# Sinkhorn attention with a leaky FFN: 96 short products ahead of q, fewer gap products, loads in halves, and a new order

## The chip, the cores and the metric

The kernel runs on one core of one Trainium2 chip. The metric is the device time in microseconds, as the median of several executions; less is better. The engines are PE (TensorE), ACT (ScalarE), DVE (VectorE), POOL (GpSimd) and SP (SyncE), and they run side by side. PE issues a weight load and a product for each matmul, and POOL and SP also issue the DMAs.

## The reference

Four batches of eight heads, 768 positions and 64 features go through an attention in which each block of 96 queries looks at one block of keys that has been mixed from all eight blocks by a normalised 8 x 8 matrix P. The result, 3072 tokens of 512 features, goes through a two-layer network with a leaky activation.

```python
P = sort_net                                   # (4, 8, 8, 8)
for _ in range(5):
    P = P - max(P, -1); P = exp(P)
    P = P / (sum(P, -1) + 1e-9)
    P = P / (sum(P, -2) + 1e-9)
k_sorted = einsum('bhij,bhjcd->bhicd', P, k_blocks)   # the same for v
scores = (q_block @ k_sorted_block.T) / sqrt(64)
attn = softmax(scores)
x = (attn @ v_sorted_block) -> (3072, 512)
h = x @ w_in                                   # 512 x 2048
g = max(h, 0) + alpha * min(h, 0)
out = g @ w_out                                # 2048 x 512
```

## The kernel before

**The work.** The 32 pairs of batch and block are called groups g (eight groups to a batch). For batch 0, q and k are turned by small PE products of 64 columns (pairs, L541; k is mixed with P in the same product through the matrix BDK), v is first copied into a padded layout (conv_v, L571, copies at L375) and then mixed (prep_v, L582), all in units that are copied out of PSUM by ACT or DVE. The matrix BDK comes from the sinkhorn steps on DVE and ACT (L490 to L505) and from spread (L514 to L527). A group of attention is: first scores (L617), row maxima on DVE (L623), for batch 0 second scores with the maxima subtracted (L638, L629), exponentials on ACT (L650, or L661 for batch 0), outputs (L672), division on DVE (L679, L682), and a transpose into xT (L697 on PE for batch 0, a DMA else). Then ffn1 (L719) multiplies xT with one of 16 tiles of w_in, ACT and DVE apply the activation (L729, L732), and ffn2 (L758) multiplies with w_out, 128 tokens at a time, in four parts; the result is copied to outstg (L375) and written out. The FFN works on chunks of two, two and then four groups.

**Loads.** They are DMAs that POOL issues, all in one queue: q, k and v of batch 0 (load_q L400, load_kv L422), w_in in four pieces of 128 rows (L793), w_out in two (L798), then what later batches need. A load converts f32 to bf16.

**The order.** Every step is put into a graph with an estimated duration, a priority and what it depends on. A list scheduler with a model of the engines then fixes the order of every engine; each engine runs its list strictly in that order. ORDER is a table with two characters for each step that shift its priority; it was found by a search.

**Gap products.** After the scheduling, `fill` walks through PE's list. Where the model sees PE idle ahead of a step, it puts products of the identity with itself there, whose results nobody reads (warm, L877). It does so in three stretches, up to the first ffn2. One such product has 256 bf16 columns and counts as 108 ns:

```python
n = int((op.start - begin) * 0.9 / unit)
if op.start <= hi and n > 0:
    x = _Op("pe", lambda e, n=n, bank=bank: make(e, n, bank), n * unit, ...)
```

The lines are those of the profile.

Of the kernel before, what the change touches and what calls it, by code (L numbers as in the profile page):

```python
# [7 lines left out]
AP = bass.AP  # L8
# [19 lines left out]
TILE_NS = 95  # L28
ORDER = (
    "W0W0W0W0W0W0W0W05GW0l3T78PEQ1K9l7Y65EIEs4XMvOvAlRW0mdJRwEqG4iGXTQOfufwMuee8gGT6cGbXokEJe4B90JCveHZicAA9jUQB1DzPFF4GGKaHc"  # L30
    "8aPHCA4nBAfy6_mlSHVedcjZcmmXi2fOu5noSXO0p4bQmukgg7JLd5XNb4k5NyqRpxOAKOZpWHdU9UOeaEbWQSrkh3-4smk4t4aqO11GW0bWNrrYNUK2Em3W"
    "2-AR7c4nBTOyEx6nE6VTT3j4j_VCppjHttlwZvlfv-kVjdpxgA_GempJzTIedlrBmB-4g0hyzlNlESMRb36rHveUTSSo_DJxhukpJSN1RQJPWXRw7D7NPepN"
    "QEhEy-6LVV39A485D4GZRj9GDA3061FN4n5GEbTSGINERVBKI9Ft7O2iRp59KrE4gJRCMWDaCESFPvKjTt9wZzLl482x11A0Da1F1NId1X4T6Q7b0m4DTr4g"
    "2i1g1eN0OeCWfkODTu5Z2C0m0m6NCN0m1r457q5cGFMvcfHJHoL_KsLa8wGqPdSBZuA_CCAIwDZHjf0mwrsWdxmhmkNeWavmxaDELyOyrUFK2lDPdQ78mbQb"
    "WuvsGKVUU6Nd-XkcdKgTYGtvjwNTp9zqg3yppVD9CnuRzjsWmqpjTvylWL2-w_ClQ0iJecrHjXVv8R9HiPVlTeWB4Z99MmHqDAu5513h5ekV4Diu363k6kJQ"
    "rZSUN2nBcMssxIy6a_v8XLqyqGhIPfj7OGV3XGhW1oogFOaIDH8o0mJVtiJxKqAp3N9JMY1sY_hrX9C4EHFH3BArWvqF3M98H4D89jGTHhINHEF_Dvf5SDFn"
    "rSSkUD3rACBFS1XdtyJ92D319yKv4PAqLpgfOu6E8oeoybjzDa7169FkRzft5Y9UOJ8hlIVreecmrQgn4HDsI9SaI0izJ56w3uW6DR1Y38MbAM8XKaJ44L7J"
    "Y7UVjbB3LoG8H5N8YZXrYHTnSaxmiheb5aGQDOQI6GXS95ZXBsJ4BFPAMBe_BAMxEPVlG9jCHM3_WfNkBp3V9WPO8baR9yGwzkzueeMe38MCadIUXl5Qcs7J"
    "DOBlN-Gn7gL14HDlT8Ez3fEPB18w9wQiIkJEFpFADrC1lvWrTZj8KzFRNf7ddav8_GsjmEakOMoYtjyUg1YMl4yry1S6stxphKsUfUqV78aYBOmolzOHlkw8"
    "Mb-biXpg895_a5RvUqk2L45-Fec_n9HPKxZCPjvWRO58F9668Ye5JUSEM26xOC3-J2JGYaSvWWfhbbQNr-sKcSPWnA_Gds_G_GiK_GpwF_ghbQPUoTSS_Gsc"  # L40
    "q4S7WnvGsUdDhK21AG4z4mGeJr9EDSIrI5RwjLKpaXL9VY3F1K1N49molEoJm119U7Amo1DbO2KKl_AYYJgfRnnEgdcwOKVxqGCPkOtLkUvryOdGph_Gj8oL"
    "udQtU3umL1WoqYTwDytNbVnVG4npnGydlwoTRPqoK25XDXGB-5rkQrL8nGpEfObklbqMUYRdMj1FMPw9SxSjdQjos7XA9WToxOntFhJ_baHhgAoXeE5R1CAq"
    "oFABUOeBHKpvWeLBcpEZ_GtJLTpVTtWIrhaEgUPZEaBFS82PEPHUFfgPdYab_4awxrhWcBexo9zxvQnrpoZYPPBx9GjLv8WhywsJ-lhx-q-t-e-ByhSbt5gx"
    "q4PEDZFbnI4QFE4k3BLt6gEHcrF6ZL1Mfhc1vgZZMQcqYuBOYI_G_GTzQOEg9EIBNH5XA7MNAH2Q9ELq1J1v553_429_7N3F0m1g6g2JUvpMJxdjNGBQSSS1"
    "H_8zbrJn1xGE3wC06DBVBG96C85Q991aHaExFVOv6pA0Cu4v7N6E6J8DAO8d96IRWcDNJ5ZF3QMTfEWUGJYABk9ZE6t9HmMG_GSVw6gnroXjyAeUdRuvVyy_"
    "YvtFRRysp0bzdEjry3ylvWu6cbpWohxbOirASrmYtQEWQAmUyk7-9_qA6aAYAxQnDBSEn8w9V1vVKHbZkJwWjzK7yrToFljrlArn3TFsgw5LBKXJlvd2nqMQ"
    "Oc6xyqlhhuQ2LQ0m303l-muwxUYcej_Gzw-nur_G_C-lq9ellKA9x8y5pUP1NYsOmosT-KqwnXejbfwxxDiNq6UfNwuZVmx7d4BBi6qqQ-BHzD-E-Cy7xRox"
    "rAtnbRIPl2WJONciriI2IXCIyydAq1pzpjhfvfeetzdHgVdvipuskrXTkovejtqSuhn7p8ybyvx-wrvprDrrwiwxxJx_z7v9vyzWoXuBxFq9qFzEy1xuyLtZ"
    "vM"
# [20 lines left out]
class _Op:  # L70
    __slots__ = ("eng", "fn", "dur", "prio", "deps", "dma", "idx", "pos", "inc", "start", "end",
                 "users", "left", "ready", "turn", "engs", "tiles")

    def __init__(self, eng, fn, dur, prio, dma, idx):
        self.eng, self.fn, self.dur, self.prio, self.dma, self.idx = eng, fn, dur, prio, dma, idx
        self.deps = set()
        self.turn = set()
        self.users = []
        self.inc = None
        self.engs = eng  # L80
        self.tiles = (0, 0)


class _Graph:
# [7 lines left out]
    def add(self, eng, fn, dur, r=(), w=(), prio=0.0, dma=None, tiles=(0, 0)):  # L92
        op = _Op(eng, fn, dur, prio, dma, len(self.ops))
        op.tiles = tiles
# [19 lines left out]
    def span(self, op, e, at, loads):  # L114

        if op.dma is None:
            d = op.dur[e] if isinstance(op.dur, dict) else op.dur
            if e == "pe":
                if op.tiles[0] and not loads[2]:
                    d += TILE_NS  # L120
                loads[2] = op.tiles[1]
            return at + d, at + d
# [22 lines left out]
    def schedule(self):  # L145
# [17 lines left out]
        loads = [0.0, 0.0, 0]  # L163
# [39 lines left out]
    def fill(self, make, unit, spans):  # L203

        out, last = [], 0.0
        for op in self.order["pe"]:
            for lo, hi, deps, bank in spans:
                begin = max([last, lo] + [self.ops[d].end + 300 for d in deps])
                n = int((op.start - begin) * 0.9 / unit)
                if op.start <= hi and n > 0:  # L210
                    x = _Op("pe", lambda e, n=n, bank=bank: make(e, n, bank), n * unit, 0.0, None, len(self.ops))
                    x.start, x.end = begin, begin + n * unit
                    x.deps.update(deps)
                    self.ops.append(x)
                    out.append(x)
# [77 lines left out]
def bass_sinkhorn_attn__then__act_prelu_kernel(  # L293
# [94 lines left out]
    d_k = [dma_sem("k%d" % n) for n in range(7)]  # L388
    d_v = [dma_sem("v%d" % n) for n in range(7)]
# [29 lines left out]
    def load_kv(t, src, name, sem, g, b, prio):  # L419
        n = 4 if b == 3 else 1  # L420
        for x in range(n):
# [3 lines left out]
                load_us / n, r=paced(g, x) * (b == 3), w=[(name, b % 2), (name, b % 2, x)] if x == 0 else [(name, b % 2, x)],  # L425
                prio=prio, dma=(sem[b + x], 700 * (b == 3 and name == "KS")))
# [7 lines left out]
    def consts():  # L434
# [25 lines left out]
        for n in range(NE):  # L460
# [13 lines left out]
              r=["identf"], w=["selk"], prio=-66)  # L474
# [33 lines left out]
    def spread(bs, prio):  # L508
# [7 lines left out]
        G.add(PE, f, 100 * n, r=["Pb", "selk"] + [("xT", 1)] * (bs[0] > 0), w=PSP, prio=prio)  # L516
# [30 lines left out]
    def prep_q(u, prio, bank):  # L547
        t, off, row, keys = bank
        G.add(PE, pairs(QS[0], 0, u, identb, 0, 128, bank), 372, r=[("QS", 0), "identb"], w=keys, prio=prio, tiles=(1, 1))
# [4 lines left out]
    def prep_k(b, u, prio, bank=BANK_P):  # L554
        n = b % 2
        t, off, row, keys = bank
        G.add(PE, pairs(KS[n], n, u, BDK, b * 128, 512, bank), 372, r=[("KS", n)] + [("KS", n, x) for x in range(4)] + [("BDK", b)], w=keys,
              prio=prio, tiles=(1, 1))
# [9 lines left out]
    def conv_v(b, u, prio):  # L568
# [3 lines left out]
              r=[("VST", b % 2)] + [("VST", b % 2, x) for x in range(4)], w=[("VD", u)], prio=prio)  # L572

    def prep_v(b, u, prio, bank=BANK_P):
# [11 lines left out]
        G.add(PE, f, 374, r=[("VD", u), "VD0", ("BDK", b)], w=keys, prio=prio, tiles=(1, 1))  # L586
# [9 lines left out]
    def attention(g, prio):  # L596
# [14 lines left out]
        def s1(e):  # L611
            inst = None
            for h4 in range(4):
# [7 lines left out]
              w=banks_s, prio=ps_, tiles=(1, 1))  # L621
# [36 lines left out]
        else:  # L658
            G.add(PE, s2, 626, r=kt_keys + qt_keys + [("nm", m), "identb"],
                  w=banks_s, prio=ps_, tiles=(1, 0))  # L660
# [15 lines left out]
        op = G.add(PE, o, t_pe(*[(65, 65)] * 8), r=vs_keys + ([("ET", me), ("ETtail", me)] if far else [("Es0", m), ("Etail", m)]), w=banks_o, prio=prio)  # L676
# [24 lines left out]
        G.add(PE, tr, t_pe(*[(96, 128)] * 4), r=[("xq", me), "identb"], w=banks_o[:1], prio=prio)  # L701
# [7 lines left out]
    def ffn1(ga, gb, ft, prio):  # L709
# [6 lines left out]
        def f(e):  # L716
            inst = None
            for kt in range(KT_TILES):
# [5 lines left out]
        op = G.add(PE, f, t_pe(*[(n, 128)] * 4), r=[("xT", g % 16) for g in range(ga, gb)] + [("w_in", kt) for kt in range(KT_TILES)],  # L724
              w=keys, prio=prio)
# [15 lines left out]
    def ffn2(t, prios):  # L741
# [11 lines left out]
        for x, (bank, key) in enumerate(banks):  # L753
            for part in range(4):
                def f(e, part=part, bank=bank, x=x):
                    inst = None
                    for ft in range(4 * part, 4 * part + 4):
# [7 lines left out]
                           + [("w_out", part // 2)], w=key, prio=prios[part] + x)  # L765
# [26 lines left out]
    for kt in range(KT_TILES):  # L792
        G.add(POOL, lambda e, kt=kt: e.dma_start(  # L793
            AP(w_in_bf, kt * DFF, [[KT_TILES * DFF, 128], [1, DFF]]),
            AP(moe_w_in.tensor, kt * 128 * DFF, [[DFF, 128], [1, DFF]])),
# [126 lines left out]
```

## Time and profile before

| | |
|---|---|
| median of 3 executions | 249.22 us (248.56 to 250.04) |
| the profiled execution | 250.91 us, of which the span from first to last instruction is 249.2 us |
| PE busy | 233.1 us, 94% of the span, 2711 products |
| PE weight loads | 140.1 us, 56% |
| DVE busy | 168.3 us, 68% |
| ACT busy | 155.2 us, 62% |
| POOL busy | 48.9 us, 20% |
| mean granted clock of TensorE | 0.993 |
| DMA | 29.81 MB, mean 120 GB/s |
| L877 (gap products) on psYP | 85 products, 14.1 us busy |
| chain that ended last | PE 85%, DVE 6%, DMA 3%, issue 3%, ACT 2% |

Times in the profile count from the first instruction. A busy PE need not be PE at its peak, since products overlap and their ends are modelled. The clock row shows the share of the full clock that TensorE was granted. An idle time that the profile puts down to "issue" is one in which the engine waited for nothing that the profile shows. The durations of a row are means of one execution.

### The profile page before, as it was taken

Reading aid. Unit: us, or ns where it says so; the run is one execution under the profiler, and the core shown is the slowest. Engines: PE = TensorE matmul, PEld = TensorE weight load, DVE = VectorE, ACT = ScalarE, POOL = GpSimd, SP = SyncE. Lnnn points to the kernel's source line nnn. Section 1 sums busy time; section 2 is a strip of 40 time slices with the busy share of each in tenths; the row PEclk is TensorE's granted clock in tenths of the full one; section 3 lists DMA queues with packets and bytes.
Section 4 is the critical chain, followed back from the end, with each engine's and each line's share of the span. In section 5 each row is a group of like instructions: output and inputs, shape, how many; then the busy total and the mean of one; then the engine's idle time right before and its main releaser. Section 6 shows DMA issues by size and latency. Waiting matters only on the chain.

```text
span 249.2 us, 6548 instructions
## 1 busy us (share of the span) xinstructions
PE 233.1 (94%) x2711; PEld 140.1 (56%) x2742; DVE 168.3 (68%) x340; ACT 155.2 (62%) x422; POOL 48.9 (20%) x70
## 2 busy tenths in 40 slices
PE   4989798989899998999999999999999999999995
PEld 3767486667655555555555555554555555555544
DVE  5777566488877887765778687654866775655520
ACT  4447355588887886746677766557676476455511
POOL 8992000064751104960000000000000000000000
PEclk9999889999999999999999999999999999999999
DMA  5999999999699899994375443213443353002103
GB/s 102 206 214 208 175 211 170 211 206 171 63 123 178 153 147 176 159 168 73 88 123 115 112 92 89 59 35 93 105 105 85 62 141 92 16 0 87 43 10 117
DMA packets 66318, 29.81 MB, mean 120 GB/s; under 512 B 58592, under 2 KB 61936, under 8 KB 66288
## 3 DMA queue, kind: packets, MB, share of 16 engines
q0 software_dynamic: 23632, 13.63, 41.8%
q1 hardware_dynamic: 42656, 15.76, 32.2%
q8 instruction: 21, 0.34, 0.6%
q14 instruction: 9, 0.07, 0.1%
HBM read 27.28 MB, written 6.29 MB: 135 GB/s over the span
## 4 chain that ended last, share of the span: by engine, by line
PE 85%; DVE 6%; DMA 3%; issue 3%; ACT 2%; POOL 0%
PE psH L719 31%; PE psYP L758 28%; PE psYP L877 4%; PE psS L758 3%; PE psO L672 3%; PE psYP L582 3%; PE psS L617 3%; PE psYP L541 2%; DMA ET<-Esb 2%; DVE hT L732 2%; PE psS L629 1%; ACT t L729 1%; PE psS L638 1%; DVE VS L375 1%; PE psO L582 1%
## 5 line engine op out<-in xcount | busy, mean ns | idle before, releaser
L732 DVE SCALAR_TENSOR_TENSOR hT<-t,omaT,psH 128x384 bf16<-128x384 f32 (+1 forms) x139 | 77.7, 571 | 39.9 <-ACT t L729 38.4
L719 PE MATMUL psH<-xT,w_in_bf 128*128 128x384 bf16 (+1 forms) x556 | 98.6, 313 | 0.2 <-DVE hT L732 0.2
L729 ACT ACTIVATE t<-psH 128x384 f32<-128x384 f32 (+1 forms) x139 | 62.6, 463 | 45.4 <-PE psH L719 43.5
L758 PE MATMUL psYP<-w_out_bf,hT 128*128 128x512 bf16 x306 | 78.2, 379 | 3.6 <-DVE hT L732 1.2
L719 PEld LDWEIGHTS psH<-xT,w_in_bf 128*128 128x128 bf16 x556 | 50.3, 98 | 32.9 <-DVE hT L732 3.6
L650 ACT ACTIVATE Esb<-psS,nf 96x96 bf16<-96x96 f32 x192 | 46.1, 343 | 5.0 <-DVE nf L623 5.0
L758 PEld LDWEIGHTS psYP<-w_out_bf,hT 128*128 128x128 bf16 x336 | 30.4, 98 | 30.1 <-DVE hT L732 1.1
L623 DVE TENSOR_REDUCE nf<-psS 96x8 f32<-96x768 f32 x24 | 22.8, 949 | 5.5 <-PE psS L617 5.4
L375 POOL COPY VD<-VST 128x384 bf16<-128x384 bf16 x15 | 14.5, 966 | 39.0 <-DMA VST<-in_v_dram 32.7
L682 DVE TENSOR_TENSOR xq<-psO,rec 96x512 bf16<-96x512 f32 x31 | 21.3, 686 | 0.9
L404 POOL DMA_DIRECT2D QN<-in_q_dram x24 | 19.8, 850 | 0.9 <-DMA xT<-xq 0.5
L877 PE MATMUL psYP<-identb 128*128 128x256 bf16 x85 | 14.1, 319 | 3.4 <-ACT identb L375 3.4
L375 ACT ACTIVATE outstg<-psYP 128x512 f32<-128x512 f32 x14 | 8.4, 597 | 7.4 <-PE psYP L758 7.4
L375 ACT ACTIVATE VS<-psYP 112x512 bf16<-112x512 f32 x14 | 9.6, 684 | 5.1 <-PE psYP L582 5.1
L582 PEld LDWEIGHTS psYP<-BDK,VD 128*64 128x64 bf16 x416 | 8.6, 111 | 6.9 <-issue 2.7
L617 PE MATMUL psS<-KT,QTz 64*128 64x96 bf16 x248 | 10.8, 205 | 1.7 <-issue 1.7
L877 PEld LDWEIGHTS psYP<-identb 128*128 128x128 bf16 x85 | 9.0, 112 | 5.7 <-ACT identb L375 3.4
L582 PE MATMUL psYP<-BDK,VD 128*64 128x64 bf16 x416 | 11.5, 198 | 0.7 <-DVE VS L375 0.7
L679 DVE RECIPROCAL rec<-psO 96x8 f32<-96x8 f32 x31 | 6.2, 199 | 7.6 <-PE psO L672 7.2
L672 PEld LDWEIGHTS psO<-VS,ET 112*128 112x128 bf16 x192 | 8.6, 98 | 4.3 <-DMA ET<-Esb 0.8
L672 PE MATMUL psO<-VS,ET 112*128 112x65 bf16 x192 | 9.9, 194 | 0.9 <-DMA ET<-Esb 0.6
L617 PEld LDWEIGHTS psS<-KT,QTz 64*128 64x128 bf16 x248 | 6.2, 94 | 6.4 <-ACT t L729 3.1
(117 smaller groups left out, 179.2 us busy)
## 6 DMA issues: line engine op xcount, KB each, us to landing
out_dram<-outstg SPq DMA_DIRECT2D x23, 256.0 KB, 2.2
KS<-in_k_dram POOLq DMA_DIRECT2D x3, 768.0 KB, 33.4
VST<-in_v_dram POOLq DMA_DIRECT2D x3, 768.0 KB, 32.5
QN<-in_q_dram POOLq DMA_DIRECT2D x24, 96.0 KB, 5.5
w_in_bf<-in_moe_w_in_dram POOLq DMA_DIRECT2D x4, 512.0 KB, 17.6
w_out_bf<-in_moe_w_out_dram POOLq DMA_DIRECT2D x2, 1024.0 KB, 28.5
QS<-in_q_dram POOLq DMA_DIRECT2D x1, 768.0 KB, 7.1
VST<-in_v_dram POOLq DMA_DIRECT2D x4, 192.0 KB, 4.5
```

The costliest lines, as they stand in the source:

```text
L375: return e.activation(o, i, ACTF.Copy) if e is nc.scalar else e.tensor_copy(o, i)
L582: inst = e.matmul(AP(t, th * 64 * row + off + dd * 64, [[row, 64], [1, 64]]), AP(VD, (8 * u + dd) * 64, [[4096, 128], [1, 64]]), AP(BDK, b ...
L617: inst = e.matmul(o, AP(QTz[n], hp * 64 * QP + h4 * 768 + i * 96, [[QP, 64], [1, 128]]), AP(KT[n], hp * 64 * ld + (h4 * 8 + i) * bk, [[ld, ...
L623: G.add(DVE, lambda e: e.tensor_reduce(AP(nx, 0, [[8, 96], [4, 2], [1, 4]]), AP(psX, 0, [[1024, 96], [512, 2], [96, 4], [1, 96]]), AxisLis ...
L650: inst = e.activation(AP(Esb[me], p * 128, [[1024, 96], [64, 2], [1, 48]]), AP(psX, (p // 4) * 512 + (p % 4) * 96, [[1024, 96], [48, 2], [ ...
L672: inst = e.matmul(AP(psZ, hp * 512 + h4 * 68, [[1024, 128], [1, 65]]), AP(ET[me] if far else Es0[m], pos(h4, hp) * 96, [[800, nk], [1, 128]]),
L682: G.add(DVE, lambda e: e.tensor_tensor(out=AP(xq[me], 0, [[512, 96], [256, 2], [64, 4], [1, 64]]), in0=AP(psZ, 0, [[1024, 96], [512, 2], [ ...
L719: inst = e.matmul(AP(pt, poff, [[1024, 128], [1, n]]), AP(w_in_bf, kt * DFF + ft * 128, [[KT_TILES * DFF, 128], [1, 128]]), AP(xT, kt * XR ...
L729: G.add(ACT, lambda e: e.activation(AP(t1[tb], 0, [[384, 128], [1, n]]), AP(pt, poff, [[1024, 128], [1, n]]), ACTF.Relu, scale=-1.0), t_ac ...
L732: G.add(DVE, lambda e: e.scalar_tensor_tensor(out=AP(hT, ft * RING + tok % RING, [[FT_TILES * RING, 128], [1, n]]), in0=AP(t1[tb], 0, [[38 ...
L758: inst = e.matmul(AP(bank[0], bank[1], [[1024, 128], [1, n]]), AP(hT, ft * RING + tok % RING, [[FT_TILES * RING, 128], [1, 128]]), AP(w_ou ...
L877: inst = e.matmul(AP(t, off, [[row, 128], [1, 256]]), identb[:, :], AP(identb, 0, [[128, 128], [0, 2], [1, 128]]))
```

## The change

- **96 short products.** PE's list now begins with 96 products of a 32-column piece of the identity with 16 columns, as soon as the identity is there. The plan counts 2.7 us for them.
- **Gap products.** A gap product now has 512 columns. After 9 us of the plan, a gap takes first as many f32 products as fit (865 ns each), then bf16 ones (216 ns each); before 9 us only bf16 ones, at 480 ns each.
- **Loads.** load_kv loads batch 0 in two column halves, and since K and V share it, V as well as K. A unit of prep_k of batch 0 depends on its own half only; conv_v depends on all pieces. w_in is loaded in eight pieces, four row blocks by two column halves, and an ffn1 tile depends on its own column half.
- **The model.** Each PE step tells how many products it has (mms). The scheduler counts two instructions for each, and lets a step that passes a border of 256 instructions wait until 5500 ns (2500 ns after 36 us of the plan) after the border before.
- **The order.** ORDER is new throughout, and the copy into selk has another priority.

```diff
+FETCH = 256
+FETCH_NS = 5500
+FETCH0 = (205, 6100.0, 449)
 ORDER = (
...
@@ span
                 loads[2] = op.tiles[1]
+                loads[3] += 2 * op.mms
+                if loads[3] > loads[5]:
+                    loads[5] += FETCH
+                    late = loads[4] + (FETCH_NS if at < 36000 else 2500) - at
+                    if late > 0:
+                        d += late
+                    loads[4] = at + (late if late > 0 else 0)
             return at + d, at + d
...
-        loads = [0.0, 0.0, 0]
+        loads = [0.0, 0.0, 0, *FETCH0]
@@ fill
-        out, last = [], 0.0
+        out, last = [head], 0.0
+        head.idx = len(self.ops)
+        self.ops.append(head)
...
-                n = int((op.start - begin) * 0.9 / unit)
-                if op.start <= hi and n > 0:
-                    x = _Op("pe", lambda e, n=n, bank=bank: make(e, n, bank), n * unit, 0.0, None, len(self.ops))
-                    x.start, x.end = begin, begin + n * unit
+                left = (op.start - begin) * 0.9
+                n = 0 if begin < 9000 else max(int(left / 865), 0)
+                m = max(int((left - n * 865) / (480 if begin < 9000 else 216)), 0)
+                if op.start <= hi and n + m > 0:
+                    x = _Op("pe", lambda e, n=n, m=m, bank=bank: make(e, n, m, bank), 0, 0.0, None, len(self.ops))
+                    x.start, x.end = begin, begin + n * 865 + m * 216
@@ load_kv
-        n = 4 if b == 3 else 1
+        n = (2, 1, 1, 4)[b]
...
-                prio=prio, dma=(sem[b + x], 700 * (b == 3 and name == "KS")))
+                prio=prio + x / 100, dma=(sem[b + x + (b > 0)], 700 * (b == 3 and name == "KS")))
@@ prep_k
-        G.add(PE, pairs(KS[n], n, u, BDK, b * 128, 512, bank), 372, r=[("KS", n)] + [("KS", n, x) for x in range(4)] + [("BDK", b)], w=keys,
-              prio=prio, tiles=(1, 1))
+        G.add(PE, pairs(KS[n], n, u, BDK, b * 128, 512, bank), 372, r=[("KS", n, x) for x in ((u // 3,) if b == 0 else range(4))] + [("BDK", b)], w=keys,
+              prio=prio, tiles=(1, 1), mms=16)
@@ ffn1
-        op = G.add(PE, f, t_pe(*[(n, 128)] * 4), r=[("xT", g % 16) for g in range(ga, gb)] + [("w_in", kt) for kt in range(KT_TILES)],
-              w=keys, prio=prio)
+        op = G.add(PE, f, t_pe(*[(n, 128)] * 4), r=[("xT", g % 16) for g in range(ga, gb)] + [("w_in", kt, ft // 8) for kt in range(KT_TILES)],
+              w=keys, prio=prio, mms=4)
@@ main
-    for kt in range(KT_TILES):
-        G.add(POOL, lambda e, kt=kt: e.dma_start(
-            AP(w_in_bf, kt * DFF, [[KT_TILES * DFF, 128], [1, DFF]]),
-            AP(moe_w_in.tensor, kt * 128 * DFF, [[DFF, 128], [1, DFF]])),
-            2750, w=[("w_in", kt)], prio=-40 + kt, dma=(dma_sem("wi%d" % kt), 0))
+    for x in range(2):
+        for kt in range(KT_TILES):
+            G.add(POOL, lambda e, kt=kt, x=x: e.dma_start(
+                AP(w_in_bf, kt * DFF + x * 1024, [[KT_TILES * DFF, 128], [1, 1024]]),
+                AP(moe_w_in.tensor, kt * 128 * DFF + x * 1024, [[DFF, 128], [1, 1024]])),
+                1375, w=[("w_in", kt, x)], prio=-40 + 4 * x + kt, dma=(dma_sem("wi%d%d" % (kt, x)), 0))
...
+    def warm(e, n, m, bank):
         t, off, row, keys = bank
         inst = None
+        for x in range(n + m):
+            ident = identf if x < n else identb
+            inst = e.matmul(AP(t, off, [[row, 128], [1, 512]]), ident[:, :], AP(ident, 0, [[128, 128], [0, 4], [1, 128]]))
         return inst
+
+    def short(e):
+        inst = None
+        for _ in range(96):
+            inst = e.matmul(AP(psYP, 0, [[1024, 32], [1, 16]]), identb[:, :32], identb[:, :16])
+        return inst
+    head = _Op("pe", short, 0, 0.0, None, 0)
+    head.deps.add(ident_op)
+    head.start = G.ops[ident_op].end + 50
+    head.end = head.start + 2700
```

## The prediction

> **What bounds the kernel now.** I read the page first: PE is busy 94% of the span, and its rows for the slices from 100 us on are nines. By stretches of time PE is busy 138.46 of 140 us between 100 and 240, and 28.45 of 30 between 70 and 100. What can be won lies in the first 70 us, so I read the timeline of PE and the chain of waits there.
>
> ```profile
> PEclk9999889999999999999999999999999999999999
> q8 instruction: 21, 0.34, 0.6%
> ```
>
> The clock row has one dip, in the fifth and sixth slices (25 to 37 us). Queue q8 carries instructions: 21 packets, 0.34 MB, so 16 KB each.
>
> ```profile
> 16.41 0.42 PE L541 MATMUL psYP<-BDK,KS 64*64 64x64 bf16 x16
> ...
> 21.38 0.22 PE L617 MATMUL psH<-KT,QTz 64*128 64x96 bf16 x2
> 21.90 0.30 PE L617 MATMUL psH<-KT,QTz 64*128 64x96 bf16 x6 [0.31 <-issue]
> ...
> 26.71 0.34 PE L617 MATMUL psS<-KT,QTz 64*128 64x96 bf16 x7
> 28.77 0.20 PE L617 MATMUL psS<-KT,QTz 64*128 64x96 bf16 x1 [1.72 <-issue]
> ```
>
> Both gaps cut one group of eight products in two, after the second and after the seventh: no data can be missing there. I counted instructions by stretches, the borders laid into the gaps.
>
> ```profile
> core 0: us, PE busy (x) PEld busy (x) DVE busy (x) ACT busy (x) POOL busy (x), PEclk, DMA share, GB/s
> 0.00:21.65 21.65, 17.13 (x349) 12.96 (x350) 15.67 (x61) 10.91 (x22) 18.85 (x33) 1.00 0.91 180
> 21.65:28.60 6.95, 5.15 (x127) 3.84 (x127) 4.00 (x8) 3.37 (x6) 0.00 (x0) 1.00 1.07 178
> ```
>
> Products plus weight loads: 699 up to the first gap, 254 between the gaps. With six and two semaphore instructions on PE that is 705 and 961, so 256 lie between them, one packet of 16 KB at 64 bytes each. So I read both gaps as PE waiting for its next block of program. Borders lie at 193 + 256n. A block seems to be asked for when PE passes the border before its own: instruction 449 ran at 16.41, the q8 packet went at 19.55 to 20.50, and 705 opened at 21.90 (5.49 us in all); 705 passed at 21.9 at the latest, the packet went at 26.15 to 27.25, and 961 opened at 28.77 (6.87). The next border asked at 28.77 and its packet started at 33.82, 5.05 later.
>
> ```profile
> 26.33:29.74 3.41, 1.69 (x25) 0.91 (x21) 1.86 (x4) 0.46 (x2) 0.00 (x0) 1.00 1.17 188
> 29.74:33.15 3.41, 3.33 (x32) 2.61 (x32) 2.04 (x7) 1.33 (x4) 0.00 (x0) 0.50 1.23 200
> ```
>
> After a stretch in which PE was busy half the time, the clock was 0.50 for 3.41 us. A stretch at 82% (16.09 to 19.50, 2.81 busy) had kept it. Last, the chain:
>
> ```profile
> 24.64 0.45 PE psS L629 x8
> 25.08 0.22 PE psYP L877 x2
> 25.30 0.38 PE psYP L672 x8
> ...
> 27.05 1.72 issue
> 28.77 0.20 PE psS L617
> ...
> 30.70 0.64 PE psH L719 x4
> 31.34 0.44 PE psS L638 x8
> 31.78 0.76 PE psS L629 x8
> 32.53 0.64 PE psH L719 x4
> ```
>
> The first attention output (L672) starts at 25.30 and the first FFN product (L719) at 30.70. That is 5.40 us, 3.68 without the gap. At half clock the three groups at 30.70, 31.34 and 31.78 and that at 32.53 take 2.48; at full clock they take 0.33, 0.28, 0.45 and 0.33 by their later rows, 1.39. So the dip costs 1.1, and gap and dip together 2.8 us: the most that this part can give.
>
> **Part by part.** *Instruction count up to the outputs.* This decides. The old kernel puts 27 + 25 + 8 + 8 + 15 gap products (166 instructions) ahead of 961. The new one puts 192 (the 96 short pairs), about five 512-column products ahead of q (10), three f32 products where 25 stood (25 x 0.108 = 2.7 us, 0.9 x 2.7 / 0.865), and some 10 to 14 instructions in the other gaps. That is about 220, 55 more. Useful instructions stay: q 192, spread 2, k 192, v 256, first scores 32, alpha 2, second scores 64, outputs 32. So PE has run about 412 when k starts at 15.38 (192 + 10 + 192 + 6 + 2, and some 10 for the gap ahead of k and the start), where the old one had 157 + 157 = 314 by the same view. Border 449 is then passed in the second k group, about 15.7 and not 16.41, and 705 opens at 15.7 + 5.49 = 21.2, 0.7 earlier. PE wants it at about 20.6, after the third v group, so that gap stays near 0.6; the copies on ACT and DVE, which set the pace from 16 to 25 us (ACT 3.95 and DVE 3.65 of 5 us between 20 and 25), hide most of it. Border 961 falls in the last second-score group (412 + 192 + 256 + 32 + 2 + 64 = 958, and some fill), ahead of both outputs, where the old kernel had both outputs before it. PE gets there at about 24.9.
>
> When it opens is not known: 21.2 + 5.49 = 26.7 or 21.2 + 6.87 = 28.1, by the two waits that the trace has. I take 26.7, since the request falls earlier, in the stretch where the loads of K, V and w_in still run as they did at 16 to 20; I keep both. Outputs at 26.7 and 3.55 us of chain (3.68 less some 0.13 at full clock) give the first FFN product at 30.25: 0.45 won. The idle time, 24.9 to 26.7, is 1.8 us where it was 1.72 plus 0.35, but further gap products are planned into the chain behind it, and so I take the clock as kept: 1.1 won. If not, that term is 0.
>
> *The head of 96.* Products of 64 columns start 0.25 us per 16 at full clock (rows of L541), 16 ns each, 31 at half: 1.5 to 3.0 us; the change plans 2.7. It lies where 27 gap products lay, hidden by the wait for QS until 9.23. If the clock is granted one 3.41 us stretch later for the weaker load, q's six groups (1.6 us) take up to 1.6 more, hidden by the sinkhorn chain on DVE, which ends at 14.22; its two casts of q lie in that chain, so 0 to 0.6. I take 0.
>
> *f32 gap products.* One lasts 0.865 by the change's own plan and cannot be cut short; no row shows one. If a gap closes early, the next step waits 0 to 0.87. Taken 0: the plan leaves a tenth of each gap free.
>
> *Loads in halves.* load_kv serves V too, so batch 0 gets four loads where two were, and w_in eight for four: six more issues on POOL at 0.53 (rows of L422 and L793), 3.2 us. The second K half goes ahead of the identity (L436 at 2.63), so the gap products start up to 0.53 later; hidden by QS. Behind the others wait VD's memset, w_out, K and Q of batch 1, and POOL's first v conversions at 16.18. The loads are 30 us deep in the queue (KS of batch 1: issue 8.16, used at 44.80), so their late issue costs nothing; the v conversions could lose 0 to 0.9, one conversion more on ACT or DVE. No k product can use the early half: k waits for BDK, ready at 15.31, not for KS. The table's offsets put w_in's first column half into six of the first eight loads and w_out's first half ahead of its last two; no FFN product waited for a weight in this trace, so 0. Shorter rows could slow the transfer: the stretch of w_out ran at 164 to 188 GB/s where K, V and w_in had 208 to 218; over 10 us of w_in that is 0 to 2, nearest to w_in itself: 0.
>
> *The order.* It is new throughout, and no row prices it. PE idles 3.69 us from 36 to 70, 1.55 to 100, 1.54 to 240. A table could save or add a fifth of these 6.8, so -1.4 to +1.4, and I take 0.
>
> *Sum*: 0.45 + 1.1 = 1.6 us. The profiled execution took 250.91 (span 249.2, 1.7 around it) and would take 249.3; from the median of 249.22 it is 247.6.
>
> [...]
>
> **The rivals.** *Border only moved (same).* The block opens at 28.1: FFN at 31.65, 0.95 lost against 1.1 of clock, 249.1. For it: the nearer request took 6.87. Also here: the clock dip falls in only some runs (the old times spread by 1.5 us, the size of that term), and then 0.45 is left, 248.8; or the gaps are something other than fetch and nothing changes, 249.2 (0.04). [...]
>
> *Slower: the outputs stand behind the block.* A request as slow as the one after 28.77 (5.05 to the packet, 0.93 for it, 1.5 until PE runs: 7.5) opens 961 at 28.7; FFN starts at 32.25, 1.55 late, and the 3.8 us of idle PE halve the clock again: 249.22 + 1.55 = 250.8. It decides from an opening at 27.15, and costs over 0.5% from 28.4. For it: the count above. Against: the first two requests were faster.
>
> **How the numbers follow.** About 0.5% (1.25 us) is what a measurement can tell here from no change. Forecast case 0.46, 247.6, its own range 245.0 (all 2.8 and 1.4 of order) to 248.0. Same 0.26. Slower 0.28, 250.5 to 252.2 with the order's 1.4. The range 245.2 to 251.4 leaves out about 0.08 above and 0.05 below.
>
> **What would show it.** Right: the second issue gap starts near 24.9, ahead of L672, and ends before 27.15; first L719 product before 30.4; no stretch at 0.50 behind it; the first q8 packet 4 us earlier than 13.48. Wrong: a gap of over 3 us ahead of L672, a later first L719 product, or PE idle from 36 to 100 us off the old 5.2 by over 1.

## The result and the profile after

The changed kernel took 253.55 us (median of 20 executions, 251.03 to 258.0), beside 251.53 us for the kernel before (20 executions, 248.56 to 254.5). The ratio is 1.0109, with a 95% interval of 1.0076 to 1.0142. A repetition, called r1 below, gave 1.0048 (1.0009 to 1.0086). It is slower, by 0.5% to 1.1%. The 249.22 us that the prediction started from was the middle of three of those executions and lay low. The ratios leave out executions over 1.5% above the fastest of their kernel, nearly all of which have a stretch at half clock, so the table of experiments gives means over all executions beside them, and the counts of such stretches below take all.

The page of the changed kernel first:

```profile
PEclk9996599999999999999999999999999999999999
q8 instruction: 22, 0.36, 0.6%
```

The page counts one more packet of program on q8 than before (r1, the same kernel again, has 21 as before), and the clock dip is deeper and earlier: slices four and five, 19 to 31 us. The timeline of PE, changed kernel (start, duration, then the group; in brackets the idle time before it and what ended it):

```profile
18.80 0.44 PE L597 MATMUL psYP<-BDK,VD 128*64 128x64 bf16 x16 [0.99 <-POOL VD L390]
...
19.95 0.28 PE L597 MATMUL psO<-BDK,VD 128*64 128x64 bf16 x5
20.53 0.35 PE L597 MATMUL psO<-BDK,VD 128*64 128x64 bf16 x11 [0.30 <-issue]
...
25.39 0.50 PE L644 MATMUL psH<-identb,nm 96*128 96x96 bf16 x4
26.44 0.50 PE L644 MATMUL psH<-identb,nm 96*128 96x96 bf16 x4 [0.55 <-issue]
...
27.16 0.65 PE L687 MATMUL psO<-VS,Es 112*128 112x65 bf16 x8
...
31.60 0.50 PE L734 MATMUL psH<-xT,w_in_bf 128*128 128x192 bf16 x4
```

Again two gaps cut a group in two with no data missing. They stand in other groups than before: one after the fifth of 16 v products, and one in the middle of the last second-score group (L644), now ahead of both outputs (L687). The first FFN product (L734) starts at 31.60; before, the same timeline had 30.50. The count by stretches, borders laid into the two gaps:

```profile
core 0: us, PE busy (x) PEld busy (x) DVE busy (x) ACT busy (x) POOL busy (x), PEclk, DMA share, GB/s
0.00:20.30 20.30, 14.67 (x349) 9.68 (x350) 14.44 (x59) 10.96 (x22) 16.31 (x29) 1.00 0.92 167
20.30:26.20 5.90, 5.36 (x128) 4.35 (x127) 3.23 (x5) 3.56 (x5) 5.90 (x10) 0.55 1.18 207
```

That is 699 and 255 products plus weight loads, against 699 and 254 before. Quite different operations stand at these places, yet the gaps come after the same number of instructions: 705 and 961. The profile of before held 0.50 for one stretch of 3.41 us (29.74 to 33.15). The clock of the changed kernel, by windows of that length laid along its steps:

```profile
14.10:17.51 3.41, 3.33 (x96) 1.99 (x90) 2.33 (x5) 2.66 (x5) 0.94 (x1) 1.00 1.04 166
17.51:20.93 3.42, 1.96 (x72) 1.36 (x72) 3.19 (x5) 2.01 (x4) 3.30 (x5) 1.00 1.14 211
20.93:24.34 3.41, 3.41 (x85) 2.82 (x79) 1.91 (x4) 2.55 (x4) 3.41 (x6) 0.50 1.16 209
24.34:27.75 3.41, 2.86 (x52) 2.17 (x49) 0.69 (x1) 1.77 (x3) 2.38 (x5) 0.50 1.23 205
```

PE was busy 1.96 of 3.42 us while it waited for POOL's conversion of v (0.99), POOL's copy of KT (0.17) and the block at 705 (0.30), and the clock was 0.50 from the next window on. Half speed lasted until 31.17, 10.24 us or three windows. The repetition r1 shows the other way to lose it; first its timeline, then its windows:

```profile
23.92 0.34 PE L644 MATMUL psH<-identb,nm 96*128 96x96 bf16 x4
26.63 0.48 PE L644 MATMUL psH<-identb,nm 96*128 96x96 bf16 x4 [2.36 <-issue]
```

```profile
23.28:26.69 3.41, 1.05 (x42) 0.79 (x35) 0.71 (x2) 1.16 (x2) 3.41 (x7) 1.00 1.24 209
26.69:30.10 3.41, 3.41 (x29) 2.17 (x30) 1.65 (x4) 1.29 (x2) 0.20 (x1) 0.50 1.18 205
```

At full clock PE reaches the border 1.6 us sooner, stands 2.36 us for the block, and loses the clock in the window after. In the chain of waits of the changed kernel's own profile, the steps from the gap to the FFN:

```profile
25.89 0.55 issue
26.44 0.50 PE psH L644 x4
...
27.37 0.44 PE psO L687 x8
...
31.70 0.41 PE psH L734 x4
```

From the first output to the first FFN product it is 4.33 us, where the prediction had 3.55: PE ran at half clock until 31.17.

**How often the clock is lost.** Each execution comes with its mean granted clock. The 10.24 us at 0.50 above are three windows, so that one takes half of 10.24 / 3, 1.707 us, off the granted time, and (1 - clock) x span / 1.707 counts the windows; the profiled execution above gives 0.021 x 249.3 / 1.707 = 3.1, the three seen. Counted so:

| kernel | executions | without a window at half clock | one | two or more |
|---|---|---|---|---|
| before (beside the experiments) | 99 | 54 | 33 | 12 |
| changed (result and r1) | 32 | 0 | 17 | 15 |

The kernel before took 249.9 to 250.1 us on average, by chip, in its executions without such a window and 251.4 to 251.8 in those with one. More than half of its executions never had the dip that its one shown profile has. The count does not say where in an execution a window lies, and the 1.7 us are all that a window by itself takes off; where executions with one window are longer by more than that, something else was lost too.

### The profile page after: what moved, and what is told of

It reads as the page before. It is cut to its first block, busy times and chain, and to the rows that moved or that the text cites. A ratio compares the mean times of both kernels' runs of the same rounds, so it can differ in the third digit from the quotient of the medians.

```text
span 249.3 us, 6654 instructions
## 1 busy us (share of the span) xinstructions
PE 236.5 (95%) x2767; PEld 138.8 (56%) x2767; DVE 167.4 (67%) x337; ACT 159.8 (64%) x425; POOL 51.9 (21%) x76
## 4 chain that ended last, share of the span: by engine, by line
PE 79%; DMA 12%; DVE 3%; POOL 2%; ACT 2%; issue 1%; POOLq 0%
PE psH L734 30%; PE psYP L773 28%; DMA VST<-in_v_dram 7%; PE psS L773 3%; DMA xT<-xq 3%; PE psO L687 3%; PE psYP L597 3%; PE psS L632 3%; DMA ET<-Esb 2%; PE psYP L556 2%; PE psS L644 1%; DVE hT L747 1%; PE psO L597 1%; PE psYP L894 1%; POOL VD L390 1%
## 5 line engine op out<-in xcount | busy, mean ns | idle before, releaser
L734 PE MATMUL psH<-xT,w_in_bf 128*128 128x384 bf16 (+1 forms) x556 | 97.2, 311 | 0.7 <-DVE hT L747 0.4
L744 ACT ACTIVATE t<-psH 128x384 f32<-128x384 f32 (+1 forms) x139 | 63.3, 463 | 42.9 <-PE psH L734 40.8
L773 PE MATMUL psYP<-w_out_bf,hT 128*128 128x512 bf16 x336 | 83.6, 379 | 1.0 <-DVE hT L747 0.9
L734 PEld LDWEIGHTS psH<-xT,w_in_bf 128*128 128x128 bf16 x556 | 49.7, 97 | 33.8 <-DVE hT L747 4.7
L773 PEld LDWEIGHTS psYP<-w_out_bf,hT 128*128 128x128 bf16 x336 | 30.9, 98 | 31.3 <-DVE hT L747 1.4
L697 DVE TENSOR_TENSOR xq<-psO,rec 96x512 bf16<-96x512 f32 x31 | 21.2, 685 | 0.9
L390 POOL COPY VD<-VST 128x384 bf16<-128x384 bf16 x15 | 13.5, 902 | 37.2 <-issue 22.1
L390 ACT ACTIVATE VS<-psYP 112x512 bf16<-112x512 f32 x16 | 11.0, 690 | 2.8 <-PE psYP L597 2.5
L390 ACT ACTIVATE outstg<-psYP 128x512 f32<-128x512 f32 x13 | 7.8, 597 | 7.6 <-PE psYP L773 7.6
L390 ACT ACTIVATE KT<-psYP 128x512 bf16<-128x512 f32 x12 | 7.2, 597 | 7.1 <-PE psYP L556 7.0
L687 PEld LDWEIGHTS psO<-VS,ET 112*128 112x128 bf16 x192 | 8.3, 98 | 3.9 <-DMA ET<-Esb 0.8
L687 PE MATMUL psO<-VS,ET 112*128 112x65 bf16 x192 | 9.9, 194 | 0.1
L773 PE MATMUL psS<-w_out_bf,hT 128*128 128x512 bf16 (+1 forms) x48 | 9.5, 344 | 0.0
```

The lines of the kernel that those rows point to most:

```text
L390: return e.activation(o, i, ACTF.Copy) if e is nc.scalar else e.tensor_copy(o, i)
L687: inst = e.matmul(AP(psZ, hp * 512 + h4 * 68, [[1024, 128], [1, 65]]), AP(ET[me] if far else Es0[m], pos(h4, hp) * 96, [[800, nk], [1, 128]]),
L697: G.add(DVE, lambda e: e.tensor_tensor(out=AP(xq[me], 0, [[512, 96], [256, 2], [64, 4], [1, 64]]), in0=AP(psZ, 0, [[1024, 96], [512, 2], [ ...
L734: inst = e.matmul(AP(pt, poff, [[1024, 128], [1, n]]), AP(w_in_bf, kt * DFF + ft * 128, [[KT_TILES * DFF, 128], [1, 128]]), AP(xT, kt * XR ...
L744: G.add(ACT, lambda e: e.activation(AP(t1[tb], 0, [[384, 128], [1, n]]), AP(pt, poff, [[1024, 128], [1, n]]), ACTF.Relu, scale=-1.0), t_ac ...
L773: inst = e.matmul(AP(bank[0], bank[1], [[1024, 128], [1, n]]), AP(hT, ft * RING + tok % RING, [[FT_TILES * RING, 128], [1, 128]]), AP(w_ou ...
```

## The experiments

There are three suspects: the instructions that the head of 96 and the gap products put ahead of the outputs, so that the block from 961 on opens too late for them; the loads in halves, which put more issues into POOL's queue; and the order. Behind the first stands a second question: is the late start of the work behind the block the loss, or the clock that PE loses while it waits?

| run | kernel | ratio to before (95%) | mean over all executions, against before, us (95%) | first output, first FFN product, us |
|---|---|---|---|---|
| before | | 1 | | 25.26, 30.50 |
| result | changed | 1.0109 (1.0076 to 1.0142) | +2.5 (±1.2) | 27.16, 31.60 |
| r1 | changed, again | 1.0048 (1.0009 to 1.0086) | +1.8 (±1.2) | 27.32, 31.31 |
| r2 | before with the new head and gap products | 1.0036 (0.9988 to 1.0083) | +2.1 (±1.3) | 27.29, 30.50 |
| r3 | before with loads in halves | 1.0102 (1.0043 to 1.016) | +2.7 (±1.7) | 29.41, 32.61 |
| r4 | changed without head and halves: the order alone | 0.9975 (0.9938 to 1.0013) | +0.1 (±1.6) | 25.07, 29.53 |
| r5 | changed without the head, old gap products | 0.9974 (0.9929 to 1.0019) | +0.9 (±1.4) | 26.91, 30.79 |
| r6 | changed with whole loads | 1.0044 (1.0007 to 1.0082) | +1.7 (±1.0) | 26.16, 30.44 |
| r7 | changed, head of 56 | 0.9937 (0.9883 to 0.9991) | 0.0 (±1.3) | 24.30, 27.63 |
| r10 | changed, head of 72 | 1.0006 (0.9958 to 1.0054) | +1.4 (±1.5) | 24.62, 29.15 |
| r8 | changed, head of 140 | 1.0036 (0.999 to 1.0083) | +1.4 (±1.2) | 27.45, 31.88 |
| r9 | head of 92, the wait filled | 1.0076 (1.0029 to 1.0123) | +1.9 (±1.1) | 26.78, 30.00 |
| r11 | head of 56 and one f32 product more | 0.9962 (0.9915 to 1.0009) | -0.4 (±1.4) | 24.23, 27.54 |
| r12 | head of 56 and whole loads | 0.9947 (0.9902 to 0.9993) | -1.8 (±1.0) | 24.32, 27.64 |

The times in the last column are from each kernel's one profile, by the timeline of PE. One profile is one execution, and not always a typical one: those of r1 and r2 are the fastest of their kernels, those of r3 and r5 the slowest. r3 was timed six times, r5 13 times, the others 12 times.

### The changed kernel again, and its parts one by one (r1 to r4)

> The changed kernel once more, for a second profile beside the one in which the clock was at half for 10.2 us. All theories: 1.1% slower than before, 1.0076 to 1.0142 as measured. Theory O (the new order loses it in the middle of the kernel): the second profile has an ordinary start, and gaps of PE that wait for a DMA between 36 and 200 us. Theory H (head and gap products): the loss stands before 36 us: the first L734 product after 31.5, and the clock at half in one to three stretches of 3.4 us. Theory L (loads in halves): the last half of V lands after 16.4 where the whole V landed at 15.9, and PE waits for the conversions of v until 18.8.

r1 is the changed kernel unedited. Its profile is shown above.

> The kernel before with its own order and loads, and only the head of 96 and the new gap products. Theory H: it has the whole loss, 1.008 to 1.014, with an issue gap after instruction 961 ahead of the first outputs. Theories O and L: 0.996 to 1.004; the gap after 961 then costs no more than the old one of 1.72 us at 27.05.

The edit puts only the head and the new rule for gap products into the kernel before:

```diff
-        out, last = [], 0.0
+        out, last = [head], 0.0
...
-                n = int((op.start - begin) * 0.9 / unit)
+                left = (op.start - begin) * 0.9
+                n = 0 if begin < 9000 else max(int(left / 865), 0)
+                m = max(int((left - n * 865) / (480 if begin < 9000 else 216)), 0)
```

In the timeline of r2, the old order's last second-score group was cut by the gap ahead of the outputs:

```profile
26.81 0.43 PE L633 MATMUL psS<-identb,nm 96*128 96x96 bf16 x6 [2.11 <-issue]
```

So the extra instructions alone bring the gap to that place, in either order: the first output moved from 25.26 to 27.29. The ratio's interval includes 1 and misses the 1.008 expected for this suspect, but over all 12 executions the mean is 2.1 us over that of the kernel before, and only one execution had no window at half clock. That one is the profile: it kept the clock in spite of the wait, and its first FFN product came no later than before (30.50), since the old gap behind the outputs was gone. Where the others lost time was not profiled.

> The kernel before with only the loads cut: K and V of batch 0 and w_in each as two DMAs of half the columns in the place of one, order of all else unchanged; a step waits for both halves. Theory L: 1.005 to 1.014, V lands 0.5 us or more later and the first outputs follow. Theories O and H: 0.997 to 1.004.

The edit keeps the old plan and issues each of K, V and w_in of the first batch as two DMAs:

```diff
-            G.add(POOL, lambda e, x=x: e.dma_start(
-                AP(t[b % 2], x * 3072 // n, [[3072, 128], [1, 3072 // n]]),
+            op = G.add(POOL, lambda e, x=x: [e.dma_start(
+                AP(t[b % 2], int(y * 3072) // n, [[3072, 128], [1, 3072 // n if b else 1536]]),
...
+                for y in ((x,) if b else (0, 0.5))],
...
+        op.parts = 2
```

It was slower by 1.0%, and its timeline shows PE waiting for POOL's conversion of v:

```profile
21.46 0.64 PE L586 MATMUL psO<-BDK,VD 128*64 128x64 bf16 x16 [2.47 <-POOL VD L377]
```

In the old order the further issues stand in POOL's queue ahead of the conversions, which began at 19.67 (before: 16.18), and the first output came at 29.41. That is far over the 0 to 0.9 us that the prediction allowed for this. It is a result on the old order, though, not yet on the change, and the profile is the slowest of six executions.

> The changed kernel's order of every engine, with whole loads (each pair of halves issued as one DMA at the earlier half's place), without the head and with the old gap products of 256 columns. Theory O: 1.008 to 1.014. Theories H and L: 0.992 to 1.004, since the sinkhorn steps end 1.6 us earlier in the new order.

The edit takes the changed kernel, puts back the old gap products and no head, and after the plan merges each pair of half loads into one DMA:

```diff
-        out, last = [head], 0.0
-        head.idx = len(self.ops)
-        self.ops.append(head)
+        out, last = [], 0.0
...
+    for pair, whole in halves.values():
+        keep, drop = sorted(pair, key=lambda o: o.start)
+        G.merge(keep, drop, whole)
```

No cost of the order by itself is seen: 0.9975, interval to both sides of 1, and a mean 0.1 us over that of the kernel before. So what makes the change slower is not the order by itself.

### The changed kernel with one part taken back (r5, r6)

> The changed kernel with its order and its loads in halves, but without the head and with the old gap products of 256 columns. Theory H (the head and the gap products put the block border after instruction 961 ahead of the first outputs, PE then stands for 2 us and the clock falls): 0.994 to 1.001 of the kernel before, outputs at about 25, first FFN product at 29.5 as in the run with the order alone. Theory L (the loads in halves cost as in the run with the loads alone): 1.004 to 1.014.

```diff
-        out, last = [head], 0.0
-        head.idx = len(self.ops)
-        self.ops.append(head)
+        out, last = [], 0.0
...
-                left = (op.start - begin) * 0.9
-                n = 0 if begin < 9000 else max(int(left / 865), 0)
-                m = max(int((left - n * 865) / (480 if begin < 9000 else 216)), 0)
+                n = int((op.start - begin) * 0.9 / unit)
```

> The changed kernel with whole loads of K, V and w_in, head and gap products kept. Theory H: 1.005 to 1.013, as the changed kernel itself; PE still stands for 1.5 to 2.5 us ahead of the first outputs, at least one stretch at half clock in nearly every execution. Theory L: 0.995 to 1.002.

```diff
+    for pair, whole in halves.values():
+        keep, drop = sorted(pair, key=lambda o: o.start)
+        G.merge(keep, drop, whole)
```

Without the head and its gap products the ratio shows no loss (0.9974), and 8 of 13 executions had no window at half clock; the mean over all, +0.9 with an interval to both sides of 0, leaves room for a part of it. With whole loads and the head the loss stays (1.0044, mean +1.7), and none of 12 executions was without such a window. So the loss goes with the head and gap products. The loads show no cost of their own in the new order: r4 and r5 differ only in them, and r6 and r1, and each pair agrees within its intervals. What cost 1% in the old order, by six executions, is not seen in the new one.

### The length of the head (r7, r8, r10)

> The changed kernel with 56 short products in the head and not 96: 80 instructions fewer, so that the border after 961 falls behind both outputs, about where the first transposes stand. Theory H by the place of the border: outputs near 25, PE stands 0.5 to 1.7 us behind them and not ahead, first FFN product near 29.5 and under 30.5; 0.992 to 1.000. If short products as such do the harm, half of them would keep more than half of the loss: 1.003 to 1.01.

> The changed kernel with 140 short products: 88 instructions more, so that the border after 961 falls into the last v groups, ahead of the second scores. Theory H: PE stands there until 705's passing (about 20.3) plus 5.5 to 6.9, 26 to 27, and the scores, exponentials and outputs follow only then: first FFN product 32.5 to 33.5, 1.012 to 1.02 of the kernel before. If more instructions early only bring the fetch forward, as the change's plan has it: no slower than with 96.

> The changed kernel with 72 short products: the border after 961 then stands at the first transpose, behind both outputs and ahead of what follows. By the place of the border: 961 is asked at about 20.3 and opens at 26 to 27, and PE wants it at about 25.7; a wait of 0.3 to 1.3, first FFN product 28 to 29, between the 27.6 of 56 and the 31.5 of 96; 0.992 to 0.999.

The edit is one number and its planned time; the ORDER stays:

```diff
-        for _ in range(96):
+        for _ in range(56):
...
-    head.end = head.start + 2700
+    head.end = head.start + 1568
```

Forty pairs fewer are 80 instructions fewer ahead of the outputs; two more gap products ahead of q make it 76. The timeline of r7:

```profile
23.72 0.51 PE L644 MATMUL psH<-identb,nm 96*128 96x96 bf16 x8
...
24.30 0.42 PE L687 MATMUL psO<-VS,Es 112*128 112x65 bf16 x8
...
27.63 0.49 PE L734 MATMUL psH<-xT,w_in_bf 128*128 128x192 bf16 x4
```

The group L644 is whole, the outputs follow at once, and the first FFN product starts 3.68 us earlier than in r1. Border 961 now falls behind the outputs, 0.28 us of start-to-start (26.91 to 27.19). The ratio fell to 0.9937, and 6 of 12 executions kept full clock. The ratio rests on these six, of 249.36 us on average. Over all 12 the mean is that of the kernel before (250.95 and 250.94), where r1 lay 1.8 us over its own: moving the border took the loss away, but a gain over the kernel before shows only where the clock was kept.

With 72 the border falls in the second output, after its sixth product, and PE stood there from 25.64 to 26.98: 1.0006, over the 0.999 expected at most. With 140 it falls back into a v group, after the second of 32 products, and PE stood from 22.32 to 25.03; it had also stood after instruction 449, from 10.52 to 11.90. That kernel took 1.0036, no slower than r1, where 1.012 to 1.02 was expected by the place of the border: with so many instructions early the block opened at 25.03, sooner than expected too. Between 56 and 96 the opening moves little (27.19, 26.98 with 72, 26.43 with 96); what changes is which operation stands behind it. The groups behind the head and the gap products, their buffers and their order are the same in all four kernels, so it is the count of instructions ahead that moved the gap.

### Late outputs or lost clock (r9, r11)

> The changed kernel with 92 short products, and two f32 gap products (some 1.9 us) ahead of the last second-score group, so that PE works through most of the time in which it waits for the block after 961. Border and outputs stay where they are, outputs at 26.5 to 27. Theory C (the half clock that the wait brings is most of the loss): the stretch at half clock around 27 to 30 is gone, executions without any such stretch come back, first FFN product near 30.3, 0.996 to 1.001. Theory D (the late outputs are the loss, whatever the clock): 1.004 to 1.01, as with 96.

```diff
-        for _ in range(96):
+        for _ in range(92):
...
+    more = {max(marked, key=lambda o: o.start).idx: 2}
...
+                if lo <= op.start <= hi:
+                    n += more.get(op.idx, 0)
```

Two f32 gap products now stand ahead of the last second-score group, so that PE is busy while the block is on its way. The timeline of r9, and from its waits of PE the one that matters later (total, times, longest):

```profile
23.31 1.98 PE L899 MATMUL psYP<-identf 128*128 128x512 f32 x4
...
26.33 0.39 PE L647 MATMUL psH<-identb,nm 96*128 96x96 bf16 x5 [0.53 <-issue]
...
30.00 0.51 PE L739 MATMUL psH<-xT,w_in_bf 128*128 128x192 bf16 x4
```

```profile
PE psO L692 <- DMA ET<-Esb: 2.2, 2, 1.9
```

The wait shrank to 0.53 us, and the clock stayed at full in this profile (mean 1.000) and in 6 of 12 executions, yet the kernel was slower than before: 1.0076. So a kept clock alone won nothing here. r7's profile, also at full clock, has a span of 245.8 us, r9's 250.4. Of these 4.6 us, 2.37 are the later first FFN product (30.00 and 27.63) and 1.9 the wait above, for the DMA transpose ET of the attention weights, the longest near 113 us, which in r7 sums to 0.3. So in this pair the late start is found again at the end, with no clock lost at all. The averages fit: the executions without a window at half clock took 251.78 us in r9, 1.64 over those of the kernel before beside it (250.14), and 249.36 in r7, 0.57 under theirs (249.93), 2.2 apart. But r9's wait for ET stands in the way of a clean answer. r1 started the FFN 1.31 us after r9 (31.31), behind a window at half clock, and its span ended 1.9 us sooner (248.5), with no wait for ET; and r9's first FFN product was no later than that of the kernel before (30.50), which r9 did not beat. What a late start costs by itself, r9 does not show.

> The changed kernel with 56 short products and one more f32 gap product (0.97 us) in the wait for the first v group, where PE stood from 17.4 to 19.0. Theory C: fewer executions with a stretch at half clock than the 6 of 12 with 56 alone; 0.989 to 0.996. If those stretches come from elsewhere (the wait for a transposing DMA near 100 us is there in both orders): 0.992 to 0.999, and as many stretches.

```diff
-        for _ in range(96):
+        for _ in range(56):
...
+    more = {min(marked, key=lambda o: o.start).idx: 1}
```

The further gap product is to cover PE's wait ahead of the first v group. Nine of 12 executions kept full clock, six in r7, but the ratio (0.9962) is no better than that of r7, and their intervals overlap widely. Whether the filling helps at all stays open.

The profile answers the other question of the expectation, whether a stretch at half clock can come from the wait for a transposing DMA. First its timeline, then its windows:

```profile
98.27 0.44 PE L599 MATMUL psYP<-BDK,VD 128*64 128x64 bf16 x16 [1.21 <-DVE KT L392]
102.56 0.62 PE L692 MATMUL psO<-VS,ET 112*128 112x65 bf16 x8 [3.85 <-DMA ET<-Esb]
```

```profile
98.91:102.32 3.41, 0.00 (x0) 0.00 (x0) 0.57 (x2) 1.26 (x2) 1.95 (x3) 1.00 1.10 90
102.32:105.73 3.41, 3.17 (x17) 1.78 (x18) 2.37 (x4) 0.49 (x1) 0.33 (x1) 0.50 0.77 185
```

The start was as good as r7's (first FFN product at 27.54, no half clock), yet the span is 251.8 us, 6.0 longer. The profiles of r3, r4 and r10 also have a window at half clock at the end of that wait or just behind it (r4: 0.50 from 104.31 to 107.72); PE stood there for 3.32, 3.57 and 1.87 us. So the windows counted for these kernels are not all the start's, and where r7's six executions lost theirs is not known.

### The best of the parts (r12)

> The changed kernel with 56 short products and whole loads of K, V and w_in. If the halves cost nothing in the new order, as the pairs with and without them say so far: the same as with 56 and halves, 0.990 to 0.998.

The edit is that of r6 and that of r7 together. Its clock row holds nines from end to end; its timeline has the first output at the place of r7's:

```profile
24.32 0.42 PE L705 MATMUL psO<-VS,Es 112*128 112x65 bf16 x8
```

It beats both kernels: 0.9947 of the kernel before, median 248.89 us beside 250.91 (the changed kernel beside its own: 253.55 to 251.53), a mean 1.8 us under that of the kernel before, and 11 of 12 executions at full clock. r7's ratio is as good, but not its mean over all executions. Whether whole loads add this to the short head, by fewer lost windows for instance, is not settled by 12 executions each on two chips.

## Why the prediction was wrong

**What the gaps are: right.** In every profile taken, the gaps from 0 to 32 us that have no data missing stand after instruction 449, 705 or 961, whatever operation is there. The first q8 packet went at 9.48, 4.00 us earlier than 13.48, as forecast. The wait at such a border cost PE 2.36 us in r1, and where the border fell decided between 0.9937 (r7) and 1.0048 (r1), or 1.8 us by the means.

**The count and the opening: right, by errors that cancel.** Border 449 fell in the second k group, as forecast, though at 14.12 and not 15.7, since k started at 13.81 rather than 15.38: the spread products, which free it, came at 12.63 rather than 14.27. Border 705 opened 6.40 us after that, at 20.53 (forecast 5.49 and 21.2), and border 961, in the forecast group, 5.90 later at 26.43, and at 26.63 in r1 (forecast 26.7, or 28.1). The first output came at 27.16 (26.7).

**The order, taken as 0: a price overlooked.** The price is near 0 in r4, but the new order changes what the late block costs. PE gets to the border at 24.26 in r1 (23.92 + 0.34), not 24.9, and r7 shows the outputs wanted at 24.30. The wait was 2.36, not 1.8, and 2.9 us of early outputs were given up, not 1.4. I measured the loss against the old kernel's outputs at 25.30, and did not ask when the new order wants them. The forecast's time of the FFN does not hang on this, since it goes from the opening; the two steps that follow are the ones that failed.

**The chain of 3.55 us: the first step that failed, mis-sized.** It was 4.33 at half clock, and 3.33 in r7 at full clock (24.30 to 27.63). With outputs 0.67 later by the chain (27.37), the first FFN product came at 31.70, not 30.25: 1.00 us later than before, not 0.45 earlier.

**The clock, +1.1: the second step that failed, with the wrong sign.** It failed twice. The forecast took the dip to be in the kernel before, while 54 of its 99 executions had no window at half clock, so that most had nothing to win; its rival "same" had named this. And it took the clock as kept, because gap products stand in the chain behind the wait. Behind it they came too late: in r1 the window with most of the wait was busy for 1.05 us and the next ran at half clock, in the first profile the clock was lost ahead of the wait, and not one of 32 executions kept full clock. The prediction had even shown the row that should have warned of this, 1.69 busy of 3.41 us ahead of the old dip; a wait of 1.8 us that falls into one window leaves 1.6. Waits of under 1 us went ahead of a loss too: in the changed kernel a window of 3.42 us with idle times of 0.99, 0.30 and 0.17 was followed by one at half clock.

**The rival "slower: the outputs stand behind the block"** had the mechanism, and the wrong condition. It was to decide from an opening at 27.15, and cost 1.55 us. The block opened at 26.43, ahead of that point, and the kernel was slower all the same, by 2.02 us (253.55 less 251.53). Its price was too low, not its place: the rival halved the clock behind the wait, as r1 shows it (0.50 from 26.69 on), but gave that no price of its own. In the profiles the FFN is 1.00 us later, and the chain at half clock alone took 0.78 more than the forecast's. That profile is the fastest of the 20 executions (251.03). Over all of them the changed kernel has on average 1.7 windows at half clock and the kernel before 0.6 (55 in 32, 57 in 99); at 1.4 to 1.6 us each, the distance of the two means of the kernel before on each chip, the 1.1 more are 1.5 to 1.8 us, an estimate. The two parts overlap, so they make no exact sum.

**The range.** Its upper end of 251.4 was drawn from a median of 249.22, which lay 2.31 us under that of the 20 executions; set on 251.53, the rival's case (+1.55) would be 253.1. Three executions of a kernel that spreads over 6 us were too few to set a range on.

**The head, the f32 products and the loads.** The head took 2.73 us (2.7), hidden, as forecast. An f32 gap product starts 0.96 to 1.05 us ahead of the next instruction, against 0.865 in the plan (which further ones in a row keep, 0.86 in r2), and holds two pairs of weight load and product, so three of them are 12 instructions where 6 were counted; the border's place came out as forecast all the same. The loads in halves show no cost in the new order, as forecast; the bound of 0.9 was wrong in the old order, where they cost 1.0%.

**PE idle from 36 to 100 us** was to show the order's share. It does not: the profile of before has 306 of the 336 products of ffn2 that the changed one records, so its 3.69 and 1.55 us of idle time are partly missing rows.

**What stays open.** The head of 56 starts the FFN 2.9 us earlier than the kernel before, but ends earlier by 1.8 us (r12) or not at all (r7) by the means. A candidate is the wait for ET: in the profiles of the new order PE stands for it 0 us (changed, r1), 0.3 (r7), 1.1 (r12), 1.5 (r6, r8), 2.0 (r5), 2.1 (r10), 2.2 (r9), 3.6 (r4) or 3.9 (r11), and in the old order 0 (r2), 0.6 (before) or 3.9 (r3). No run took that wait away. And how the loss of the changed kernel splits between late start and clock was not measured apart: r9 kept the clock in its profile, but waited for ET.

## What to carry to other kernels

Count the instructions of the engine ahead of its first dependent chain, and find where the borders of its program blocks fall (every 256 instructions in these runs): a filler that is free in time can still be dear in instructions. Here 40 short pairs more put a border ahead of the outputs, 1.0048 (r1) beside 0.9937 (r7). Compare a late start with when the new order wants the work, not with when the old one did it. Before a term is credited for a dip or a stall, see in how many executions it is there; one profile is one execution.

## What the runs showed of the hardware

- A block of 256 instructions opened 5.5 to 6.9 us after PE passed the border before it, in every profile where PE stood waiting for it in the first 30 us (5.49 and 6.87 in the kernel before, 6.40 and 5.90 in the changed one, 6.02 in r1, from 20.61 to 26.63). The packets on q8 that these waits ended with took 0.9 to 1.1 us, and PE went on 1.2 to 1.6 us after their end. PE can run the 256 instructions in less: in r1 it took 3.45 us from the opening at 20.61 to the start of instruction 961 at 24.06.
- A window of 3.41 us with PE busy for 1.96 us was followed by one at half clock (0.50, changed kernel, from 20.93), as were those with 1.69 (before, from 29.74) and 1.05 (r1, from 26.69). One with 2.81 was not (before, 16.09 to 19.50), and in r10 neither was one with 1.97 (16.82 to 20.24 us), so the busy time of a window does not settle it alone. Nor does the length of a wait: r2's profile kept the full clock in spite of 2.11 us. What settles it stays open.
- A window at half clock stood at the end of a wait for a DMA near 100 us as well: of 3.85 us in r11 (0.50 from 102.32 to 105.73), and just behind one of 1.87 in r10.
- An f32 product of 512 columns shows as two pairs of weight load and product, and starts 0.96 to 1.05 us ahead of the next instruction, or 0.86 behind another of its kind (r2).
